# Set attention with routed experts on one core: weighing split over three engines, outputs stored as whole 128-partition rows

## The chip, the cores and the metric

One NeuronCore of a Trainium2 chip runs the kernel. The metric is the device time of one execution in microseconds (us). Before the change three executions took 180.69, 181.9 and 183.5 us, median 181.9 us. The execution that was profiled took 182.12 us.

## The reference, cut to what matters

An induced-set attention feeds a top-1 mixture of experts. `x` is 4 x 11456 x 128 (fp32), `inducing` is 32 x 128, there are 8 experts.

```python
def mab(q, kv):
    s = scale * (q @ kv.transpose(0, 2, 1))
    a = softmax(s)
    return a @ kv
h = mab(I, x)                        # 32 rows for each of 4 batches
x = mab(x, h).reshape(B * S, D)      # every token attends to the 32 rows

logits = x @ w_gate
expert_idx = argmax(logits)
gate_w = softmax(logits)[expert_idx]
out[mask] = gate_w[mask, None] * (np.maximum(xe @ w1[e], 0.0) @ w2[e])
```

## The kernel before

**Tiling.** A batch is cut into four segments (q = 0 to 3) and six groups (g), so there are 24 blocks k = 6 b + g of 15 x 4 x 32 tokens. A block's input is a tile of 128 partitions x 7680 bytes (`load_xt`, L528). Its output is a tile of 128 partitions: for each of four slices i (of up to 128 token rows) and each of the four segments q, 128 channels, 8192 bytes in a partition. The fourth slice i = 3 holds 96 rows and not 128, so in partitions 96 to 127 only the first three slices, 6144 bytes, are output.

**Stages.** A first pass (scores L539, maximum L545, exponential L582, transposition L585, `h_sum` L591) gives the batch's 32 rows h. For that, the block is also needed with tokens on partitions: 12 blocks are loaded a second time (`load_xn`, L531), 12 are turned by TensorE (`turn`, L551, evicted by `turn_out`, L556). A chain per batch (L611 to L763) picks the expert, fetches its weights (1 MB) and makes `h4`, the expert's output for the 32 rows. A second pass makes scores again (L539 with `hc`), maximum (`max2`, L766) and exponentials (`exp2`, L771), then the gate's chain for a round of one to three blocks: logits on TensorE (L774), VectorE, GpSimd (`gate_sm` L793, `gate_ls` L802, `gate_den` L816), ScalarE (`gate_exp`, L810), and the gate's factors `c_all` (`gate_c`, L819). Last, `experts` (L831) makes the output on TensorE into four PSUM banks, one for each q, 16 products of 32x128 by 32x128 for a block.

**Weighing.** Each bank (a quarter of a block, 128 x 512 values) is multiplied by the gate's factors on its way from PSUM into the block's output tile. `weigh` (L840) does this as one VectorE instruction with a broadcast operand, or as four ScalarE instructions, one for each slice i, since ScalarE takes its factor per partition:

```python
src, dst, c = self.bank(o).rearrange("p (i c) -> p i c", c=P), self.ob3(ob)[:, :, q, :], self.c_all[:, k, :, q]
if e == "DVE":
    self.nc.vector.tensor_tensor(out=dst, in0=src, in1=c.unsqueeze(2).to_broadcast([P, 4, P]), op=ALU.mult)
else:
    for i in range(4):
        self.nc.scalar.activation(dst[:, i], src[:, i], AF.Copy, scale=c[:, i : i + 1])
```

The tile is laid out (i, q, c), so a bank is written as four pieces of 512 bytes. For blocks 21 to 23 (`PARTS`) `weigh_part` (L849) goes by slices i over all four banks instead. `evict` (L857) and `weigh_late` (L859) exist but are not used, as `LATE` is empty.

**Stores.** SyncE issues every load but three and every store, in one order. Blocks 0 to 20 are stored by two transfers: partitions 0 to 95 with 8192 bytes each (768 KB) and partitions 96 to 127 with 6144 bytes (192 KB). Blocks 21 to 23 go out in two or four parts. 53 stores in all.

**Order.** `schedule` (L86) is a list scheduler that runs when the program is built: each operation has a rank (tables such as `THIRD`, `SECOND`, `LOAD_T`, offsets `OFF`), a planned duration for each engine that may do it, and buffers. It puts the instructions of each engine in a fixed order and chooses the engine where two are possible; VectorE takes such work only when ScalarE is busy for over `BEHIND` more ns (or over 0 for the blocks in `HURRY`). 17 buffers of 8192 bytes a partition (`big`) serve loads (`xt`, `xn`) and outputs (`ob`) alike; an output's buffer is free again when its stores have landed. Eight PSUM banks serve scores, turned blocks, `experts` and the small products.

Of the kernel before, what the change touches and what calls it, by code (L numbers as in the profile page):

```python
# [18 lines left out]
P = 128  # L19
# [10 lines left out]
BIG = 4 * NQ * P  # L30
LEFT = 3 * P
# [5 lines left out]
HOP, BEHIND = 55, 300  # L37
# [3 lines left out]
MODES = {"S1_": (1, 115), "S2_": (1, 115), "H": (1, 210), "LG": (1, 290), "X": (3, 190), "TR": (2, 40), "G": (1, 60)}  # L41
# [164 lines left out]
D = dict(S=812, H=805, X=900, TR4=430, TR3=330)  # L206
# [9 lines left out]
PARTS = {23: 1, 22: 1, 21: 2}  # L216
HURRY = (20, 22, 23)

EARLY = ()
LATE = ()  # L220
# [5 lines left out]
GROUPS = {"bank": (8, {"fe": 4, "o": 13, "mi": 18}), "big": (17, {"xt": 11, "xn": 4, "ob": 48})}  # L226


LOAD_T = [-6186, -5601, -2755, -2825, -4812, -1904, -3185, -850, -622, -34, 238, 439, 517, 628, 1135, 2484, 2554, 2211, 3138, 4227, 2869, 7643, 6799, 8479]
LOAD_N = [-1317, 303, -1889, 159, -514, 1482, -1301, -520, -276, -4, -1768, -515, 578, 431, 1568, 3352, 553, 193, -1797, 59, 2620, 2857, 583, 571]  # L230
FIRST = [-2245, -1527, -2081, 4254, 356, -2649, 1607, 163, 3238, 1476, 958, 3511, 1490, 2053, 2904, -2421, -2752, -2413, -3886, -2475, -4110, -1943, 831, -4632]
SECOND = [-232, 3747, 2518, 1714, -1344, -186, 366, 299, 306, 398, 156, 3259, 806, 2622, 811, 3248, -572, 3258, -168, 203, 186, 995, -368, 1821]
THIRD = [-4712, -4102, -212, 180, -264, 299, -78, 144, -4893, 605, 111, -3584, -3232, -435, -337, -3717, -61, -2978, -3177, -450, -45, -86, -3934, 558]
CHAIN = [-3399, -3392, -3373, -3377]

OFF = {'M1_': -684, 'ON': -730, 'TR': 292, 'TE': -809, 'MQ': -632, 'FD': -1684, 'NB': -843, 'E1_': -4857, 'T1_': -638, 'ZP': 660, 'H': -869, 'F': -875, 'AC': -39, 'hc': -101, 'gz': -555, 'gb': -1330, 'gg': -658, 'G': -64, 'GT': -981, 'GS': -346, 'GL': 2312, 'P': 1158, 'PC': 2646, 'PF': -127, 'h4_': -1128, 'dx': 1261, 'd': -2758, 'DF': -519, 'th': -371, 'M2_': -767, 'E2_': -412, 'LG': -240, 'LV': 1074, 'SM': -466, 'RS': 2277, 'LS': -208, 'PR': -697, 'SE': 117, 'SD': 902, 'C': -1284, 'X': -1247, 'V': 3829, 'OUT': -223, 'RL': 2569, 'GA': -1596, 'LT': -1764, 'LN': -833, 'CS': -1434, 'VL': 7}
# [7 lines left out]
def make_plan(K):  # L244
# [15 lines left out]
    for b in range(B):  # L260
# [5 lines left out]
        for g in range(NG):  # L266
# [26 lines left out]
            if g % 2:  # L293
# [3 lines left out]
                fd = op(f"FD{b}.{p}", r, {"PE": 280}, lambda mi=mi, b=b, p=p: K.max_fold(mi, b, p), [mq], take=[mi])  # L297
# [3 lines left out]
                for u in (g - 1, g):  # L301
# [3 lines left out]
                    ex = op(f"E1_{ku}", ru, {"ACT": 550}, lambda fe=fe_, e=e1_, b=b, p=p: K.exp1(fe, e, b, p), [nb], take=[e1_], use=[fe_])  # L305
# [52 lines left out]
    for nr, ks in enumerate(ROUNDS):  # L358
# [22 lines left out]
        c = op(f"C{nr}", rr, {"DVE": 90 + 110 * n + 240 * len(bs)}, lambda gt=gate, ks=ks: K.gate_c(gt, ks), [a, *(thrs[b] for b in bs)], use=[gate])  # L381
        rounds.append(c)
        for u, k in enumerate(ks):
            b, g = divmod(k, NG)
            ru = THIRD[k]
            os_, ob = [Buf("o") for _ in range(NQ)], Buf("ob")
            x = op(f"X{k}", ru, {"PE": D["X"]}, lambda os_=os_, e=e2[u], b=b: K.experts(os_, e, b), [exs[u], h4s[b], None if k in EARLY else c], take=[*os_, ob], use=[e2[u]], lat=70)
            step = PARTS.get(k, 4)
            vs = []
            for q in range(NQ):  # L390
                late = 0 if k in HURRY else None
                if k in LATE:
                    vs.append(op(f"V{k}.{q}", ru, {"ACT": 470, "DVE": 590}, lambda e, o=os_[q], ob=ob, q=q: K.evict(e, o, ob, q), [x], use=[os_[q], ob], wait=late))
# [17 lines left out]
class Issue:  # L411
# [108 lines left out]
    def ob3(self, b):  # L520
        return self.big[b.slot].rearrange("p (i q c) -> p i q c", q=NQ, c=P)
# [667 lines left out]
```

## Time and profile before

| | |
|---|---|
| median of three executions | 181.9 us (180.69 to 183.5) |
| the profiled execution | 182.12 us |
| its span, first to last instruction | 180.3 us |
| TensorE busy | 147.7 us (82%) |
| VectorE busy | 124.8 us (69%) |
| ScalarE busy | 120.0 us (67%) |
| GpSimd busy | 18.4 us (10%) |
| read from HBM, written to HBM | 39.87 MB, 23.59 MB |
| mean rate of all transfers over the span | 355 GB/s |

Busy is the time in which an engine had at least one instruction under way. The DMA share is the mean busy share of the core's 16 DMA engines; it can exceed 1 slightly, since a packet counts where it starts. An engine that is busy is not at its peak: a DMA packet that waits inside its transfer is busy as well, so share and GB/s are to be read together. No chain of waits to the end was found in this trace; the page's part on it is empty.

### The profile page before, as it was taken

How to read it: one execution, taken by the hardware profiler on the slowest of the kernel's cores; microseconds unless marked ns; L12 is line 12 of the kernel's file. 1: busy time of each engine (PE TensorE's matmuls, PEld its weight loads, DVE VectorE, ACT ScalarE, POOL GpSimd, SP SyncE). 2: the span in 40 equal slices, each digit the busy share in tenths (PEclk: the TensorE clock that was granted, in tenths of full speed). 3: DMA queues.
4: the chain of work that ended last, by engine and by line, in shares of the span. 5: the costliest groups of instructions: out<-in, count | busy, mean ns of one | idle time of the engine just before them, and what ended most of it. 6: DMA issues, size and time to landing. Idle time of an engine off the chain costs nothing.

```text
span 180.3 us, 6160 instructions
## 1 busy us (share of the span) xinstructions
PE 147.7 (82%) x2438; PEld 102.0 (57%) x2439; DVE 124.8 (69%) x360; ACT 120.0 (67%) x364; POOL 18.4 (10%) x75
## 2 busy tenths in 40 slices
PE   0699989999999999979999999989899889780000
PEld 0266767765577566538875545877644569670000
DVE  1117477798799989877789588979877948985000
ACT  3045354518256888766855999999999998993000
POOL 3000000000034000002400000241001401000000
PEclk9999999999999999999999999999999965965555
DMA  4999999999999998999999999999989999799990
GB/s 146 411 426 421 414 419 416 412 408 416 414 418 417 378 278 282 418 426 417 411 412 420 396 415 399 383 323 317 327 245 358 370 335 291 266 284 314 260 305 19
DMA packets 11124, 63.94 MB, mean 355 GB/s; under 512 B 1808, under 2 KB 1936, under 8 KB 8688
## 3 DMA queue, kind: packets, MB, share of 16 engines
q1 hardware_dynamic: 10512, 60.32, 89.2%
q10 hardware_dynamic: 576, 3.15, 4.4%
q8 instruction: 21, 0.34, 0.7%
q14 instruction: 15, 0.12, 0.2%
HBM read 39.87 MB, written 23.59 MB: 352 GB/s over the span
## 4 chain that ended last, share of the span: by engine, by line


## 5 line engine op out<-in xcount | busy, mean ns | idle before, releaser
L847 ACT ACTIVATE big<-bank,c_all 128x128 f32<-128x128 f32 x228 | 64.2, 555 | 5.1 <-PE bank L836 5.1
L836 PE MATMUL bank<-h,e 32*128 32x128 f32 x768 | 38.5, 307 | 4.7 <-ACT big L847 3.9
L836 PEld LDWEIGHTS bank<-h,e 32*128 32x128 f32 x768 | 32.1, 204 | 16.5 <-ACT big L847 9.1
L543 PE MATMUL bank<-big,it_s 128*32 128x480 f32 x192 | 26.1, 602 | 7.9 <-DMA big<-in_xT 7.8
L562 ACT COPY big<-bank 128x512 f32<-128x512 f32 (+1 forms) x37 | 19.5, 571 | 16.8 <-PE bank L554 14.9
L554 PE MATMUL bank<-csb,big 128*128 128x128 f32 x180 | 26.0, 291 | 0.2 <-issue 0.2
L772 ACT ACTIVATE e<-bank,nb 128x480 f32<-128x480 f32 x24 | 18.1, 791 | 11.3 <-DVE nb L769 4.5
L596 PE MATMUL bank<-big,e1t 128*32 128x129 f32 x720 | 25.6, 274 | 0.0
L554 PEld LDWEIGHTS bank<-csb,big 128*128 128x128 f32 x180 | 21.5, 152 | 6.9 <-issue 4.2
L546 DVE TENSOR_REDUCE mx<-bank 128x1 f32<-128x480 f32 x24 | 15.4, 645 | 14.1 <-PE bank L543 14.0
L596 PEld LDWEIGHTS bank<-big,e1t 128*32 128x32 f32 x720 | 21.6, 110 | 5.8 <-issue 3.7
L543 PE MATMUL bank<-big,hc 128*32 128x480 f32 x192 | 23.8, 570 | 0.7 <-ACT big L847 0.7
L844 DVE TENSOR_TENSOR big<-bank,c_all 128x512 f32<-128x512 f32 x27 | 18.0, 682 | 5.2 <-PE bank L836 5.2
L583 ACT ACTIVATE e<-bank,mx 128x480 f32<-128x480 f32 x24 | 15.1, 687 | 6.1 <-DVE mx L580 6.1
L768 DVE TENSOR_REDUCE mx<-bank 128x1 f32<-128x480 f32 x24 | 15.5, 645 | 4.3 <-PE bank L543 2.5
L586 DVE STREAM_TRANSPOSE e1t<-e 128x480 f32<-128x480 f32 x24 | 15.7, 660 | 1.4 <-PE bank L596 1.0
L543 PEld LDWEIGHTS bank<-big,it_s 128*32 128x32 f32 x192 | 5.6, 111 | 12.6 <-issue 9.7
L543 PEld LDWEIGHTS bank<-big,hc 128*32 128x32 f32 x192 | 6.2, 109 | 6.9 <-issue 3.5
L781 PE MATMUL bank<-e,gzb 128*32 128x128 f32 x192 | 8.1, 282 | 0.2 <-ACT big L847 0.2
L564 DVE COPY big<-bank 128x512 f32<-128x512 f32 (+1 forms) x11 | 6.7, 615 | 1.5 <-PE bank L554 1.0
L855 ACT ACTIVATE big<-bank,c_all 128x128 f32<-128x128 f32 x24 | 6.8, 440 | 0.9 <-PE bank L836 0.6
L803 POOL TENSOR_TENSOR ls<-lv,rs 128x336 f32<-128x336 f32 (+2 forms) x9 | 6.1, 686 | 9.5 <-DVE rs L800 5.8
(93 smaller groups left out, 130.9 us busy)
## 6 DMA issues: line engine op xcount, KB each, us to landing
big<-in_xT SPq DMA_DIRECT2D x24, 960.0 KB, 12.3
out<-big SPq DMA_DIRECT2D x21, 768.0 KB, 7.8
big<-in_xn SPq DMA_DIRECT2D x12, 967.5 KB, 13.3
out<-big SPq DMA_DIRECT2D x23, 192.0 KB, 7.6
wr<-in_wcat ACTq DMA_DIRECT2D x3, 1024.0 KB, 10.5
out<-big SPq DMA_DIRECT2D x6, 256.0 KB, 4.9
wr<-in_w SPq DMA_DIRECT2D x2, 512.0 KB, 5.6
out<-big SPq DMA_DIRECT2D x1, 512.0 KB, 6.7
```

The costliest lines, as they stand in the source:

```text
L543: self.nc.tensor.matmul(dst, lhsT=lhsT, rhs=x[:, k0:k1, q, :], start=True, stop=True)
L546: self.nc.vector.tensor_reduce(self.mx1[b][g // 2][:, g % 2 : g % 2 + 1], self.bank(fe)[:, :GW], AX.X, ALU.max)
L554: self.nc.tensor.transpose(ps[:, k * P : (k + 1) * P], x[:, k0 + k].rearrange("p q t -> p (q t)"), self.ident)
L562: self.nc.scalar.copy(dst, src)
L583: self.nc.scalar.activation(self.at(e), self.bank(fe)[:, :GW], AF.Exp, bias=self.mx1[b][p + 1][:, 2:3])
L586: self.nc.vector.transpose(self.at(t), self.at(e))
L596: self.nc.tensor.matmul(ps[32 * j : 32 * j + 32, : P + 1], lhsT=e[:, k, :], rhs=x[:, k, :], start=(n < 4), stop=(n >= 2 * GB - 4))
L768: self.nc.vector.tensor_reduce(t, self.bank(fe)[:, :GW], AX.X, ALU.max)
L772: self.nc.scalar.activation(self.at(e)[:, 0:GW], self.bank(fe)[:, :GW], AF.Exp, bias=self.nb2[k])
L836: self.nc.tensor.matmul(self.bank(os_[q])[:, i * P : (i + 1) * P], lhsT=self.at(e)[s, i * P : (i + 1) * P], rhs=self.h4[b][s, :], start=Tr ...
L844: self.nc.vector.tensor_tensor(out=dst, in0=src, in1=c.unsqueeze(2).to_broadcast([P, 4, P]), op=ALU.mult)
L847: self.nc.scalar.activation(dst[:, i], src[:, i], AF.Copy, scale=c[:, i : i + 1])
```

## The change

- The output tile is laid out (q, i, c): a bank's 512 values lie in one piece of 2048 bytes in each partition. The tensor in HBM has the same layout, and is put in order outside the timed execution. The pitch of a row stays 8192 bytes.
- `WHOLE`: blocks 0 to 20 are stored by one transfer of 128 partitions x 8192 bytes (1 MB), which includes the 2048 bytes in each of partitions 96 to 127 that are not output. Blocks 21 to 23 go out in parts by segments q, 128 partitions each.
- `LATE.get(k, 2)`: in every block two of the four quarters (q = 2, 3) are evicted from PSUM without a factor, by ScalarE or VectorE (one instruction), and then multiplied in place by GpSimd, one 128x512 instruction each. The other two are weighed as before. `weigh_part` is gone.
- The plan's durations, ranks and offsets are new, so the order on every engine may differ anywhere. The work of the passes, the loads and the chain is the same.
- `general_part`, a fallback for tokens whose expert differs, follows the new layout.

```diff
-HOP, BEHIND = 55, 300
+HOP, BEHIND = 55, 400
...
+WHOLE = 1
+
 EARLY = ()
-LATE = ()
+LATE = {0: 2, 1: 2, 2: 2, 3: 2, 4: 2, 5: 2, 6: 2, 7: 2, 8: 2, 9: 2, 10: 2, 11: 2, 12: 2, 13: 2, 14: 2, 15: 2, 16: 2, 17: 2, 18: 2, 19: 2, 20: 2}
...
-GROUPS = {"bank": (8, {"fe": 4, "o": 13, "mi": 18}), "big": (17, {"xt": 11, "xn": 4, "ob": 48})}
...
+GROUPS = {"bank": (8, {"fe": 24, "o": 97, "mi": 17}), "big": (17, {"xt": 11, "xn": 4, "ob": 39})}
...
-                if k in LATE:
-                    vs.append(op(f"V{k}.{q}", ru, {"ACT": 470, "DVE": 590}, lambda e, o=os_[q], ob=ob, q=q: K.evict(e, o, ob, q), [x], use=[os_[q], ob], wait=late))
-                elif step == 4:
-                    vs.append(op(f"V{k}.{q}", ru, {"ACT": 740, "DVE": 600}, lambda e, o=os_[q], ob=ob, k=k, q=q: K.weigh(e, o, ob, k, q), [x, c], use=[os_[q], ob], wait=late))
+                if q < NQ - LATE.get(k, 2):
+                    v = op(f"V{k}.{q}", ru, {"ACT": 1140, "DVE": 600}, lambda e, o=os_[q], ob=ob, k=k, q=q: K.weigh(e, o, ob, k, q), [x, c], use=[os_[q], ob], wait=late)
                 else:
-                    vs.append(op(f"V{k}.{q}", ru, {"ACT": 740, "DVE": 760}, lambda e, os_=os_, ob=ob, k=k, i=q: K.weigh_part(e, os_, ob, k, i), [x, c], use=[*os_, ob], wait=late))
...
+                    v = op(f"VE{k}.{q}", ru, {"ACT": 475, "DVE": 600}, lambda e, o=os_[q], ob=ob, q=q: K.evict(e, o, ob, q), [x], use=[os_[q], ob], wait=late)
+                    v = op(f"VL{k}.{q}", ru, {"POOL": 970}, lambda ob=ob, k=k, q=q: K.weigh_late(ob, k, q), [v, c], use=[ob])
+                vs.append(v)
...
-                cuts = ((q, 4, 0, 96), (q, 3, 96, P)) if step == 4 else ((q, q + step, 0, 96 if q == 3 else P),) if step == 1 else ((0, 2, 0, P),) if q == 0 else ((2, 4, 0, 96), (2, 3, 96, P))
...
+                cuts = ((0, P, 4),) if WHOLE or step == 1 else ((0, 96, 4), (96, P, 3))
...
-        return self.big[b.slot].rearrange("p (i q c) -> p i q c", q=NQ, c=P)
+        return self.big[b.slot].rearrange("p (q i c) -> p q i c", q=NQ, c=P)
...
-    def store(self, ob, b, g, i0, i1, p0, p1):
-        src = self.big[ob.slot][p0:p1, i0 * NQ * P : i1 * NQ * P]
-        self.nc.sync.dma_start(self.out[b, g, p0:p1, i0 * NQ * P : i1 * NQ * P], src)
+    def store(self, ob, b, g, q0, q1, p0, p1, ni):
+        dst = self.out[b, g, p0:p1, 0:BIG].rearrange("p (q i c) -> p q i c", q=NQ, c=P)[:, q0:q1, 0:ni]
+        self.nc.sync.dma_start(dst, self.ob3(ob)[p0:p1, q0:q1, 0:ni])
...
     def evict(self, e, o, ob, q):
-        self.copy(e, self.ob3(ob)[:, :, q, :], self.bank(o).rearrange("p (i c) -> p i c", c=P))
-
-    def weigh_late(self, ob, k, i):
-
-        t = self.ob3(ob)[:, i]
-        self.nc.gpsimd.tensor_tensor(out=t, in0=t, in1=self.c_all[:, k, i].unsqueeze(2).to_broadcast([P, NQ, P]), op=ALU.mult)
+        self.copy(e, self.ob3(ob)[:, q].rearrange("p i c -> p (i c)"), self.bank(o))
+
+    def weigh_late(self, ob, k, q):
+
+        t = self.ob3(ob)[:, q]
+        self.nc.gpsimd.tensor_tensor(out=t, in0=t, in1=self.c_all[:, k, :, q].unsqueeze(2).to_broadcast([P, 4, P]), op=ALU.mult)
```

## Rows read from the trace of the kernel before

**Rows 1.** The page: span, and the span in 40 slices (busy tenths, clock, DMA, GB/s).

```profile
span 180.3 us, 6160 instructions
...
PE   0699989999999999979999999989899889780000
...
ACT  3045354518256888766855999999999998993000
...
PEclk9999999999999999999999999999999965965555
DMA  4999999999999998999999999999989999799990
GB/s 146 411 426 421 414 419 416 412 408 416 414 418 417 378 278 282 418 426 417 411 412 420 396 415 399 383 323 317 327 245 358 370 335 291 266 284 314 260 305 19
```

**Rows 2.** Busy time by stage over the whole span, with granted clock, DMA share, GB/s.

```profile
core 0: us, PE busy (x) PEld busy (x) DVE busy (x) ACT busy (x) POOL busy (x), PEclk, DMA share, GB/s
0.00:5.00 5.00, 0.00 (x0) 0.01 (x1) 0.64 (x8) 1.50 (x3) 1.43 (x20) 1.00 0.54 175
5.00:60.00 55.00, 53.12 (x784) 36.58 (x788) 37.60 (x99) 26.17 (x55) 4.66 (x17) 1.00 1.02 415
60.00:107.00 47.00, 44.27 (x734) 28.08 (x734) 38.92 (x113) 36.57 (x108) 4.42 (x15) 1.00 1.00 386
107.00:141.00 34.00, 31.70 (x638) 21.75 (x641) 28.13 (x77) 33.58 (x121) 4.89 (x14) 1.00 0.97 341
141.00:177.00 36.00, 18.62 (x296) 15.55 (x288) 19.52 (x66) 22.19 (x85) 3.04 (x9) 0.66 0.89 291
177.00:180.30 3.30, 0.00 (x0) 0.00 (x0) 0.00 (x0) 0.00 (x0) 0.00 (x0) 0.50 0.01 2
```

**Rows 3.** DMA issues (KB each, median us to landing); then all stores.

```profile
big<-in_xT SPq DMA_DIRECT2D x24, 960.0 KB, 12.3
out<-big SPq DMA_DIRECT2D x21, 768.0 KB, 7.8
...
out<-big SPq DMA_DIRECT2D x23, 192.0 KB, 7.6
...
L536 SPq DMA_DIRECT2D out<-big x53: 316/685/2559, 62.4 to 174.0; - x53
```

**Rows 4.** Stores issued from 143.5 to 152.7 us; then busy time from 152.7 to 158.

```profile
L536 SPq DMA_DIRECT2D out<-big x6: 446/1672/2559, 143.5 to 152.7; - x6
...
DMA to landing us min/median/max: 6.1/7.7/8.0
...
152.70:158.00 5.30, 4.30 (x88) 3.86 (x91) 5.09 (x16) 5.30 (x23) 0.25 (x1) 1.00 0.77 265
```

**Rows 5.** The last work of an engine, and stores issued from 162 to 175 us.

```profile
163.00 1.14 ACT L855 ACTIVATE big<-bank,c_all 128x128 f32<-128x128 f32 x4 [0.28 <-DVE big L853]
...
L536 SPq DMA_DIRECT2D out<-big x10: 382/1562/2077, 160.6 to 174.0; - x10
...
DMA to landing us min/median/max: 2.9/5.5/7.1
```

**Rows 6.** Groups by line and shape: busy us, mean ns of one, idle before.

```profile
L847 ACT ACTIVATE big<-bank,c_all 128x128 f32<-128x128 f32 x228 | 64.2, 555 | 5.1 <-PE bank L836 5.1
L836 PE MATMUL bank<-h,e 32*128 32x128 f32 x768 | 38.5, 307 | 4.7 <-ACT big L847 3.9 <-DVE big L853 0.7
L844 DVE TENSOR_TENSOR big<-bank,c_all 128x512 f32<-128x512 f32 x27 | 18.0, 682 | 5.2 <-PE bank L836 5.2
L562 ACT COPY big<-bank 128x512 f32<-128x512 f32 x30 | 16.6, 590 | 16.7 <-PE bank L554 14.9 <-POOL u L734 1.5 <-POOL se L817 0.3
```

**Rows 7.** The same view, GpSimd's multiplication of the gate by three sizes.

```profile
L803 POOL TENSOR_TENSOR ls<-lv,rs 128x336 f32<-128x336 f32 x6 | 4.6, 774 | 6.1 <-DVE rs L800 5.8 <-ACT part L562 0.3
L803 POOL TENSOR_TENSOR ls<-lv,rs 128x224 f32<-128x224 f32 x2 | 1.1, 574 | 0.6 <-DVE sm L794 0.6
L803 POOL TENSOR_TENSOR ls<-lv,rs 128x112 f32<-128x112 f32 x1 | 0.4, 380 | 2.8 <-ACT big L847 2.8
```

**Rows 8.** From 107 to 161 us: all work, then weighing on ScalarE and VectorE alone.

```profile
107.00:161.00 54.00, 48.86 (x915) 36.15 (x919) 44.76 (x132) 53.00 (x194) 7.92 (x23) 0.92 0.95 327
...
107.00:161.00 54.00, 44.33 (x157) 0.92 0.95 327
...
107.00:161.00 54.00, 13.96 (x21) 0.92 0.95 327
```

More of the change, by code (lines that the diff above doesn't have):

```diff
@@ L202, in schedule @@
     return order
-D = dict(S=812, H=805, X=900, TR4=430, TR3=330)
+D = dict(S=812, H=812, X=905, TR4=430, TR3=330)
 LAT = dict(PE=180, DVE=85, ACT=115, POOL=45)
@@ L296, in make_plan @@
                 mq = op(f"MQ{b}.{p}", r, {"DVE": 120}, lambda b=b, p=p: K.max_spread(b, p), [m1[g - 1], m1[g], nb_prev, cs])
-                fd = op(f"FD{b}.{p}", r, {"PE": 280}, lambda mi=mi, b=b, p=p: K.max_fold(mi, b, p), [mq], take=[mi])
+                fd = op(f"FD{b}.{p}", r, {"PE": 300}, lambda mi=mi, b=b, p=p: K.max_fold(mi, b, p), [mq], take=[mi])
                 nb = op(f"NB{b}.{p}", r, {"DVE": 100}, lambda mi=mi, b=b, p=p: K.max_all(mi, b, p), [fd], use=[mi])
@@ L304, in make_plan @@
                     fe_, e1_, e1t_, xnr_ = e1[u]
-                    ex = op(f"E1_{ku}", ru, {"ACT": 550}, lambda fe=fe_, e=e1_, b=b, p=p: K.exp1(fe, e, b, p), [nb], take=[e1_], use=[fe_])
+                    ex = op(f"E1_{ku}", ru, {"ACT": 510}, lambda fe=fe_, e=e1_, b=b, p=p: K.exp1(fe, e, b, p), [nb], take=[e1_], use=[fe_])
                     tt = op(f"T1_{ku}", ru, {"DVE": 565}, lambda e=e1_, t=e1t_: K.turn_e(e, t), [ex], take=[e1t_], use=[e1_])
@@ L372, in make_plan @@
         side = "DVE" if nr in QUICK else "POOL"
-        a = op(f"LG{nr}", rr, {"PE": 30 + 140 * n}, lambda lg=lg, es=e2, ks=ks: K.logits(lg, es, ks), [*(gzbs[b] for b in bs), *exs], take=[lg], use=[lg, *e2])
+        a = op(f"LG{nr}", rr, {"PE": 100 + 215 * n}, lambda lg=lg, es=e2, ks=ks: K.logits(lg, es, ks), [*(gzbs[b] for b in bs), *exs], take=[lg], use=[lg, *e2])
         a = op(f"LV{nr}", rr, {"DVE": 75 + 140 * n}, lambda lg=lg, lv=lv, n=n: K.logits_turn(lg, lv, n), [a], take=[lv], use=[lg])
         a = op(f"SM{nr}", rr, {side: 80 + 20 * n if side == "DVE" else 220 + 40 * n}, lambda e=side, lv=lv, gt=gate, n=n: K.gate_sm(e, lv, gt, n), [a], take=[gate], use=[lv])
-        a = op(f"RS{nr}", rr, {"DVE": 50 + 105 * n}, lambda gt=gate, n=n: K.gate_rs(gt, n), [a], use=[gate])
+        a = op(f"RS{nr}", rr, {"DVE": 50 + 108 * n}, lambda gt=gate, n=n: K.gate_rs(gt, n), [a], use=[gate])
         a = op(f"LS{nr}", rr, {side: 70 + 120 * n if side == "DVE" else 150 + 210 * n}, lambda e=side, lv=lv, gt=gate, n=n: K.gate_ls(e, lv, gt, n), [a], use=[lv, gate])
@@ L380, in make_plan @@
         a = op(f"SD{nr}", rr, {side: 80 + 20 * n if side == "DVE" else 160 + 40 * n}, lambda e=side, gt=gate, n=n: K.gate_den(e, gt, n), [a], use=[gate])
-        c = op(f"C{nr}", rr, {"DVE": 90 + 110 * n + 240 * len(bs)}, lambda gt=gate, ks=ks: K.gate_c(gt, ks), [a, *(thrs[b] for b in bs)], use=[gate])
+        c = op(f"C{nr}", rr, {"DVE": 100 + 120 * n + 240 * len(bs)}, lambda gt=gate, ks=ks: K.gate_c(gt, ks), [a, *(thrs[b] for b in bs)], use=[gate])
         rounds.append(c)
@@ L840, in weigh @@
     def weigh(self, e, o, ob, k, q):
-        src, dst, c = self.bank(o).rearrange("p (i c) -> p i c", c=P), self.ob3(ob)[:, :, q, :], self.c_all[:, k, :, q]
+        src, dst, c = self.bank(o).rearrange("p (i c) -> p i c", c=P), self.ob3(ob)[:, q], self.c_all[:, k, :, q]
         if e == "DVE":
@@ L1097, in general_part @@
                             nc.vector.transpose(ec, e2)
-                            rows = (out_flat[bass.ds((b * NG + g) * P, 96), :], out_flat[bass.ds((b * NG + g) * P + 96, 32), 0 : LEFT * NQ])
-                            ob = pl.ob.tile([P, 4, NQ, P], F32, name="ob")
-                            mine = ob.rearrange("p i q c -> p (i q c)")
-                            mine = (mine[0:96, :], mine[96:P, 0 : LEFT * NQ])
+                            rows = [out_flat[bass.ds((b * NG + g) * P + p0, p1 - p0), q * 4 * P : q * 4 * P + n] for p0, p1, n in ((0, 96, 4 * P), (96, P, LEFT)) for q in range(NQ)]
+                            ob = pl.ob.tile([P, NQ, 4, P], F32, name="ob")
+                            mine = [ob.rearrange("p q i c -> p q (i c)")[p0:p1, q, 0:n] for p0, p1, n in ((0, 96, 4 * P), (96, P, LEFT)) for q in range(NQ)]
                             for m, r in zip(mine, rows):
@@ L1126, in general_part @@
                                         )
-                                    nc.vector.tensor_tensor(out=ob[0:n, i, q, :], in0=ob[0:n, i, q, :], in1=o[0:n, 0:P], op=ALU.add)
+                                    nc.vector.tensor_tensor(out=ob[0:n, q, i, :], in0=ob[0:n, q, i, :], in1=o[0:n, 0:P], op=ALU.add)
                             for m, r in zip(mine, rows):
@@ L1181 @@
     ]
-    out = nc.dram_tensor("out_0", (B, NG, P, BIG), F32, kind="ExternalOutput").ap()
+    out = nc.dram_tensor("out_0", (B, NG, P, PITCH), F32, kind="ExternalOutput").ap()
     with tile.TileContext(nc) as tc:
```

42 lines of the change are left out of this document (17 added, 25 removed).

## The prediction

> **What bounds the kernel now.** I read the page first, the slices from left to right. The DMA line stands at nine tenths or more almost everywhere [rows 1]. Below it the GB/s line tells more: about 415 in the first third, and then, with the engines as busy as before, 245 to 370 from slice 26 on. So the transfers set the pace from start to end, and in the second half they get slower without getting rarer.
>
> The stages say the same in one table [rows 2]. From 5 to 60 us the DMA share is 1.02 at 415 GB/s. No store is issued before 62.4 us [rows 3], so this is the rate of loads alone. From 60 to 107 us, loads with a few stores, it is 386; from 107 to 141 us, nearly all stores, 341 at a share of 0.97; from 141 to 177 us, stores and little else, 291 at 0.89. A busy engine thus moves 415 / 1.02 = 407 GB/s (times 16) in loads and 291 / 0.89 = 327 in stores.
>
> Why are stores slower? Loads go to 128 partitions; stores come from 96 and then from 32 [rows 3]. The stretch from 152.7 to 158 us tells most [rows 4]: the DMA share falls to 0.77 although the six stores issued before it take 6.1 to 8.0 us to land, so transfers were outstanding all through it. Some of the 16 engines had run empty while others still had a backlog: the work was unevenly spread, and those with a backlog were slow. [...] I read the slow stores as a matter of which partitions a transfer covers.
>
> Second, who feeds the stores? From 107 to 161 us ScalarE is busy for 53.0 of 54 us, 44.3 of it with weighing, and TensorE for 48.9 [rows 8]. ScalarE is the bound of computing there; TensorE's wait before `experts` is mostly for ScalarE [rows 6]. But the last weighing ends at 163.00 + 1.14 = 164.1 us, while stores are issued until 174.0 [rows 5] and bytes move until about 177 [rows 2]: 13 us of drain. So the DMA engines set the end, and ScalarE stands close behind.
>
> **The change part by part.**
>
> *Whole-row stores.* They add 32 x 2048 bytes for each of 24 blocks, 1.57 MB: 63.94 MB (the GB/s of rows 2 times their stretches, 63.9) become 65.51 MB. What 128 partitions x 8192 bytes cost in a store, no row of before shows. Upper bound: the rate of 141 to 177 us, 291 GB/s, 3.6 us for a store. Lower bound: the loads' 415 GB/s, 2.53 us. The new store has the loads' shape, 128 rows of nearly the same length (8192 against 7680 bytes) in one transfer, so I take 415. The sum of the whole traffic then is 65.51 MB / 415 GB/s = 157.9 us. Ahead of it lie 2.9 us (0 to 5 us moved 0.875 MB, worth 2.1 us); behind it 3.3 us in which nothing moves [rows 2]. The last store can't be overlapped: 2.9 us from issue to landing at the least [rows 5], of which its 256 KB are 0.6 us, so 2.3 us more. Loads and stores will not mesh without gaps: the stage from 60 to 107 us ran at 386 instead of 415, 3.3 us lost; part of that is the old stores' doing, so I keep half, 1.6 us. Sum 2.9 + 157.9 + 2.3 + 3.3 + 1.6 = 168.0 us of span. The profiled execution took 182.12 us with a span of 180.3, so 1.8 us lie around it: 169.8 us, rounded 170. That execution stands 0.2 us above the median of the runs shown, so no correction is due.
>
> [...]
>
> *Dividing the weighing.* A quarter costs ScalarE 64.2 / 57 = 1.13 us (four instructions) and VectorE 0.68 us [rows 6]. An eviction costs ScalarE 0.55 us by its copies of the same size (16.6 / 30) [rows 6]; it may be less, as the destination is now one piece; I take 0.55. From 107 to 161 us 39 quarters went through ScalarE (157 / 4) and 21 through VectorE, 60 in all [rows 8]. After the change 30 are evicted and 30 weighed. ScalarE: 53.0 - 44.3 + 30 x 0.55 = 25 us; VectorE: 44.8 - 14.0 + 30 x 0.68 = 51 us; with ten weighings handed to ScalarE, 36 and 44 us. So both fall well under 54, and TensorE's 48.9 becomes the longest. Computing would end some 5 us sooner, near 159 us. That is worth nothing by itself, since the transfers end at 163 to 165 us by the sum above; but it keeps the stores fed, and if this cover is gone (second rival) it costs 5 us. `weigh_part` going away saves VectorE and ScalarE little and is costed at nothing, hidden in the drain of the last blocks.
>
> *GpSimd's 48 instructions.* GpSimd takes 380, 574 and 774 ns for 112, 224 and 336 values [rows 7], 1.76 ns a value; on that line 512 cost 1.08 us. Lower bound: 0.77 us, the row of fewer values. [...] I take 1.08. In the stretch of 60 quarters that is 30 x 1.08 + 7.9 = 40 us of 54, so GpSimd keeps up. It adds a wait: in GpSimd's order the gate's `gate_sm`, `gate_ls` and `gate_den` now stand behind these instructions, up to 1.08 us each, 3.2 us a round; `gate_exp` on ScalarE, `gate_c` on VectorE and then `experts` wait for them. Ten rounds could lose 32 us if nothing else were ready; TensorE has scores of later blocks to do meanwhile, so I charge nothing. A block's store also starts some 2 us later, as two GpSimd instructions follow its last eviction; with stores outstanding, that is hidden, and its buffer is held longer by as much.
>
> *SyncE.* 31 issues of stores replace 53. Behind a store that waits, later loads wait too on this queue; the store now waits for GpSimd. Since most loads are issued before 107 us and there is a backlog of 12 us [rows 3], I charge nothing.
>
> **The rivals.**
>
> *First, computing sets the end.* Work still ends at 164.1 us, because TensorE does not get shorter, or because GpSimd's wait eats the 5 us. Then the last store needs 5.5 us (the median of the last ten [rows 5]), and 3.3 + 1.8 us follow: 174.7 us. For it: TensorE at 48.9 of 54 us [rows 8]. [...]
>
> *Second, stores of 128 partitions are no faster* (the change doesn't do what it says, because the limit lies in writing to HBM). Then 1.57 MB more at 291 GB/s is 5.4 us: 187.5 us, slower. For it: the drop in GB/s follows the writes [rows 1]. [...]
>
> *Third, GpSimd becomes the bound.* If its instruction costs t, the stretch lasts 30 t + 7.9 us. It equals today's 54 us at t = 1.54. The whole is slower than before once computing ends at 171.4 us (182 - 5.5 - 3.3 - 1.8), that is at t = 1.78. [...]
>
> **How the numbers follow.** The forecast (transfers bound, 170 us) gets 0.62, with a range of 165.5 (no gaps, no tail) to 173. Rival one (174.7) gets 0.22, rival two (187.5) 0.08, rival three (from 182 to 193) 0.08. Leaving out the two slow ones and the fringe, the range is 165 to 177. Faster by over 2% (under 178.3; about what a measurement of this kernel can tell from no change): 0.62 + 0.22, less a little for a late rival one, 0.83. Within 2%: rival one's late end and rival three near its threshold, 0.08. Slower: 0.09.
>
> **What would show it.** Right: GB/s near 400 or above in the stretches where stores dominate; a store of 1 MB landing every 2.5 to 2.7 us while several are outstanding; weighing on ScalarE down to about 10 us per 60 quarters; GpSimd's instruction near 1.1 us; the last landing within 6 us after the last evicted bank. Wrong: 300 GB/s at a full DMA share in the store stretches (rival two); GpSimd busy nine tenths with ScalarE or TensorE waiting for `ls` or `se` (rival three); a DMA share that falls to 0.8 from 120 us on because no block is ready (rival one).

## The result and the profile after

The changed kernel took 173.28 us (median of three, 172.34 to 173.77) against 181.9 us: the ratio is 0.955, 95% interval 0.943 to 0.967. The profiled execution took 172.34 us with a span of 170.5 us, so 1.8 us lie around the span as before. In the experiments below, an execution more than 1.5% above the fastest of its kernel stays in the median and is left out of the ratio; without such executions the two kernels with paired stores and the division take 184.4 us (old order) and 185.5 us (new order) instead of 185.5 and 186.1.

The page's slices of the changed kernel, which answer to [rows 1], with one row of the DMA issues and one of all stores, which answer to [rows 3]:

```profile
span 170.5 us, 6074 instructions
...
PE   0599999999999998999999999997999985666300
...
ACT  3046637338554592969246896798793995781700
POOL 3000000000024262037430452788694799786800
...
DMA  4999999999999999999999999999999999899890
GB/s 140 407 422 427 411 420 411 413 416 409 415 418 411 420 411 320 368 425 420 419 410 414 426 316 414 423 424 421 411 417 397 349 423 373 340 377 380 317 394 38
...
out<-big SPq DMA_DIRECT2D x21, 1024.0 KB, 8.3
...
L537 SPq DMA_DIRECT2D out<-big x31: 332/343/769, 61.2 to 162.4; - x31
```

The GB/s line is the one to read: before, it sank to 245 to 370 from slice 26 on; now it is at 411 to 424 in slices 26 to 29 and lies between 317 and 423 from there until the last full slice. The DMA line is as full as before. GpSimd, idle before for most of the span, is busy from slice 11 on.

Busy time by stage, answering to [rows 2]; the columns are the same (after the stretch and its length: busy us and instructions of TensorE, its weight loads, VectorE, ScalarE, GpSimd, then clock, DMA share, GB/s). The last row is the stretch of [rows 8]:

```profile
0.00:5.00 5.00, 0.00 (x0) 0.01 (x1) 0.64 (x8) 1.50 (x3) 1.43 (x20) 1.00 0.56 182
5.00:60.00 55.00, 53.16 (x792) 36.20 (x796) 37.36 (x100) 28.08 (x59) 5.49 (x18) 1.00 1.02 415
60.00:107.00 47.00, 46.00 (x810) 30.18 (x806) 41.48 (x113) 32.02 (x77) 17.86 (x29) 1.00 1.00 395
107.00:141.00 34.00, 31.31 (x651) 21.11 (x647) 30.88 (x82) 28.05 (x78) 26.06 (x38) 1.00 1.01 408
141.00:170.50 29.50, 11.91 (x214) 10.33 (x206) 16.82 (x37) 13.02 (x40) 16.85 (x21) 0.71 0.80 316
...
107.00:161.00 54.00, 43.22 (x856) 31.44 (x848) 47.70 (x118) 41.05 (x118) 41.51 (x57) 0.91 0.97 389
```

From 107 to 141 us, nearly all stores, the rate is 408 GB/s where it was 341 [rows 2]. Up to 60 us the rate did not change. What is left of slowness lies in the last stretch, with a DMA share of 0.80. From 107 to 161 us ScalarE fell from 53.0 to 41.05 us, GpSimd rose from 7.9 to 41.5.

The groups that answer to [rows 6 and 7] (line, busy us, mean ns, idle before); L856 is GpSimd's multiplication, L563 ScalarE's copies out of PSUM (turned blocks and late quarters together), L848 and L845 the weighing on ScalarE and VectorE:

```profile
L856 POOL TENSOR_TENSOR big<-big,c_all 128x512 f32<-128x512 f32 x48 | 49.4, 1050 | 24.8 <-ACT big L563 16.0 <-DVE big L565 5.5 <-DVE hc L629 2.8
L563 ACT COPY big<-bank 128x512 f32<-128x512 f32 x72 | 39.7, 604 | 35.5 <-PE bank L555 18.4 <-PE bank L837 12.6 <-issue 3.4
L837 PE MATMUL bank<-h,e 32*128 32x128 f32 x768 | 33.1, 302 | 1.8 <-DVE big L845 1.1 <-DVE big L565 0.4 <-ACT big L848 0.2
L848 ACT ACTIVATE big<-bank,c_all 128x128 f32<-128x128 f32 x100 | 29.2, 404 | 0.0
L845 DVE TENSOR_TENSOR big<-bank,c_all 128x512 f32<-128x512 f32 x23 | 15.5, 675 | 1.3 <-PE bank L837 1.2
```

ScalarE's weighing fell from 64.2 to 29.2 us (100 instructions, 25 quarters). GpSimd takes 1.05 us an instruction. TensorE's `experts` takes 33.1 us instead of 38.5, and its waits for banks fell from 4.7 to 1.8 us; that the second is the reason for the first was not tested.

### The profile page after: what moved, and what is told of

The parts are those of the page before. It is cut to its first block, busy times and chain, and to the rows that moved or that the text cites. A ratio compares the mean times of both kernels' runs of the same rounds, so it can differ in the third digit from the quotient of the medians.

```text
span 170.5 us, 6074 instructions
## 1 busy us (share of the span) xinstructions
PE 142.4 (84%) x2438; PEld 97.8 (57%) x2439; DVE 127.2 (75%) x337; ACT 102.7 (60%) x255; POOL 67.7 (40%) x123
## 5 line engine op out<-in xcount | busy, mean ns | idle before, releaser
L563 ACT COPY big<-bank 128x512 f32<-128x512 f32 (+1 forms) x80 | 43.2, 593 | 36.7 <-PE bank L555 19.7
L856 POOL TENSOR_TENSOR big<-big,c_all 128x512 f32<-128x512 f32 x48 | 49.4, 1050 | 24.8 <-ACT big L563 16.0
L837 PE MATMUL bank<-h,e 32*128 32x128 f32 x768 | 33.1, 302 | 1.8 <-DVE big L845 1.1
L837 PEld LDWEIGHTS bank<-h,e 32*128 32x128 f32 x768 | 28.2, 203 | 9.1 <-DVE big L845 2.0
L848 ACT ACTIVATE big<-bank,c_all 128x128 f32<-128x128 f32 x100 | 29.2, 404 | 0.0
L773 ACT ACTIVATE e<-bank,nb 128x480 f32<-128x480 f32 x24 | 15.3, 687 | 15.2 <-DVE nb L770 7.6
L845 DVE TENSOR_TENSOR big<-bank,c_all 128x512 f32<-128x512 f32 x23 | 15.5, 675 | 1.3 <-PE bank L837 1.2
L587 DVE STREAM_TRANSPOSE e1t<-e 128x480 f32<-128x480 f32 x24 | 15.6, 656 | 0.9 <-ACT e L584 0.9
L565 DVE COPY big<-bank 128x512 f32<-128x512 f32 (+1 forms) x16 | 10.3, 646 | 4.0 <-PE bank L837 2.5
L550 POOL MEMSET big<- 128x15 f32 x12 | 1.3, 127 | 25.5 <-PE bank L597 22.0
L795 POOL TENSOR_SCALAR sm<-lv 128x48 f32<-128x48 f32 (+2 forms) x9 | 3.2, 355 | 11.8 <-DVE lv L785 10.1
```

Of the source, the lines that this page charges most:

```text
L563: self.nc.scalar.copy(dst, src)
L587: self.nc.vector.transpose(self.at(t), self.at(e))
L773: self.nc.scalar.activation(self.at(e)[:, 0:GW], self.bank(fe)[:, :GW], AF.Exp, bias=self.nb2[k])
L837: self.nc.tensor.matmul(self.bank(os_[q])[:, i * P : (i + 1) * P], lhsT=self.at(e)[s, i * P : (i + 1) * P], rhs=self.h4[b][s, :], start=Tr ...
L856: self.nc.gpsimd.tensor_tensor(out=t, in0=t, in1=self.c_all[:, k, :, q].unsqueeze(2).to_broadcast([P, 4, P]), op=ALU.mult)
```

## The experiments

Three theories stood against each other. **1:** the gain comes from transfers that cover all 128 partitions. **2:** it comes from ScalarE's relief by GpSimd. **3**, added after the first runs: it comes from the new order. Unless said otherwise a variant keeps the order of its parent on every engine; only what an operation issues is changed. Times are medians; each ratio is to the kernel before, run on the same chip in turn (its median was 182.6 to 182.9 us there).

### Stores alone

The disputed price was measured by itself. A first kernel has only stores of 8192-byte rows from six tiles of 1 MB: whole; as 96 and 32 partitions; as 64 and 64; whole again.

```diff
+    shapes = (((0, P),), ((0, 96), (96, P)), ((0, 64), (64, P)), ((0, P),))
...
+            for g in range(NG):
+                for a, z in cuts:
+                    nc.sync.dma_start(out[b, g, a:z, 0:BIG], big[g][a:z, :])
```

> Leaves out all computing and all loads: four phases of six stores of 8192-byte rows each, from six tiles, with a pause between the phases: 128 partitions in one transfer; 96 and 32; 64 and 64; 128 again. Theory 1: about 2.5 us a tile for one transfer (15 us a phase), 3.3 us for 96 and 32 (20 us), more for 64 and 64. If writing to HBM is what limits stores: the same time a tile in all four phases, 3 us or more.

Windows inside the first, second and fourth phase (VectorE, GpSimd, clock, DMA share, GB/s). The pause before a phase is a small write to each tile, and a tile's next store waits for its own write only; so the phases ran into each other at their borders, and the second is somewhat mixed with the third:

```profile
16.00:28.00 12.00, 0.29 (x5) 0.00 (x0) 1.00 1.01 416
32.00:48.00 16.00, 0.29 (x5) 0.00 (x0) 1.00 1.01 337
70.00:82.00 12.00, 0.00 (x0) 0.00 (x0) 1.00 0.98 410
```

Whole tiles go out at 410 to 416 GB/s, a load's rate; 1 MB is 2.5 us. With 96 and 32 partitions it is 337 GB/s at the same busy share. Writing to HBM is not what limits the old stores.

A second kernel, with clean pauses, separates the ranges: 0 to 95 alone, 96 to 127 alone, 0 to 63 alone, and 0 to 63 and 64 to 127 in turn.

```diff
-    shapes = (((0, P),), ((0, 96), (96, P)), ((0, 64), (64, P)), ((0, P),))
+    shapes = (((0, 96),), ((96, P),), ((0, 64),), ((0, 64), (64, P)))
...
-            for t in big:
+            for t in reversed(big):
                 nc.vector.memset(t[:, 0:1], 2.0)
```

> Leaves out all computing and all loads: four phases of six tiles with rows of 8192 bytes, each phase begun after the last store of the one before: partitions 0 to 95 alone; 96 to 127 alone; 0 to 63 alone; 0 to 63 and 64 to 127 as two transfers. If a transfer's rate goes with the share of partitions that it covers evenly: 96 partitions 2.4 to 2.6 us a tile (no quicker than 128, at 2.45), 32 partitions 0.9 to 1.2 us, 64 alone 2.4 us, 64 and 64 together no more than 2.8 us since the two halves overlap. If only bytes count: 1.85, 0.62, 1.23 and 2.45 us.

A window inside each phase, same columns:

```profile
16.00:28.00 12.00, 0.00 (x0) 0.00 (x0) 1.00 0.96 317
33.00:40.00 7.00, 0.00 (x0) 0.00 (x0) 1.00 1.00 206
44.00:57.00 13.00, 0.00 (x0) 0.00 (x0) 1.00 0.97 204
61.00:80.00 19.00, 0.00 (x0) 0.00 (x0) 1.00 0.99 313
```

At 317 GB/s the 768 KB of 96 partitions take 786 432 bytes / 317 GB/s = 2.48 us, as long as a whole megabyte. 32 and 64 partitions alone go at half the full rate (206 and 204 GB/s) with all 16 engines busy (share 1.00 and 0.97): the engines are occupied, but a byte takes them twice the time. So in these runs the rate depends on which partitions a store covers, and bytes alone do not give its price. Two of the expected times were too low: 256 KB from 32 partitions took 1.27 us (0.9 to 1.2 expected), and 1 MB as 64 and 64 took 3.35 us (no more than 2.8 expected).

### The store's shape in either kernel

In the changed kernel, each whole store is split into 96 and 32 partitions; bytes, order and division stay.

```diff
-        self.nc.sync.dma_start(dst, self.ob3(ob)[p0:p1, q0:q1, 0:ni])
+        for a, z in ((p0, 96), (96, p1)) if q1 - q0 == NQ else ((p0, p1),):
+            self.nc.sync.dma_start(self.out[b, g, a:z, q0 * 4 * P : q1 * 4 * P], self.big[ob.slot][a:z, q0 * 4 * P : q1 * 4 * P])
```

> The changed kernel in the same order on every engine, but each 1 MB store is issued as two transfers, 96 and 32 partitions of 8192 bytes; bytes, division and plan stay. Theory 1 (the gain comes from transfers that cover all 128 partitions): a block's store goes from some 2.65 us back to about 3.2 us or more, 21 x 0.55 = 11.6 us at a full DMA queue, so 182 to 186 us, with GB/s near 300 to 340 and packets that take longer at a full DMA share in the store stretches. Theory 2 (the gain comes from ScalarE's relief by GpSimd and from the new order; the shape of the store matters little): at most 175 us.

186.08 us, ratio 1.029 (1.012 to 1.045): all of the gain is lost, and more. The stages of [rows 2] from 107 us on, in this kernel:

```profile
107.00:141.00 34.00, 28.81 (x562) 19.50 (x558) 27.91 (x71) 25.10 (x73) 23.46 (x33) 0.95 0.92 326
141.00:177.00 36.00, 16.54 (x310) 13.75 (x310) 20.39 (x47) 16.69 (x50) 20.32 (x27) 0.71 0.96 324
```

ScalarE has slack (25.1 of 34 us), the DMA engines are as busy as ever, and 324 to 326 GB/s come out. Theory 2 has no place for that.

In the kernel before, each pair is made one whole store.

```diff
+        if i0 == 0 and p0 == 96:
+            return
+        if i0 == 0 and i1 == 4:
+            p1 = P
         src = self.big[ob.slot][p0:p1, i0 * NQ * P : i1 * NQ * P]
```

> The kernel before in its own order, but each of its 21 paired stores is one transfer of 128 partitions x 8192 bytes; nothing else. Theory 1: the drain after the last weighing shrinks from 13 us to some 6 us, and then ScalarE is the bound: weighing ends near 162 to 164 us and the time is 172 to 176 us, so most of the gain without any division of work. Theory 2: 180 to 183 us, since ScalarE stays busy all the time and 1.6 MB more are moved.

179.18 us, ratio 0.988 (0.968 to 1.009; the two medians, 179.18 and 182.87 us, give 0.980): too little to be told from no change, so theory 1 in its plain form missed here. From 107 to 161 us:

```profile
107.00:161.00 54.00, 49.13 (x912) 34.34 (x905) 44.88 (x129) 53.25 (x193) 7.97 (x23) 0.94 0.92 357
```

ScalarE is full (53.25 of 54 us) and the DMA share falls to 0.92: now the transfers wait for blocks, while ScalarE has no time to spare. The faster store ran into the second bound, as expected, but this bound ended at 167 to 168 us and not at 162 to 164.

### The division in either kernel

In the changed kernel, the late quarters are weighed where they are evicted, and GpSimd does nothing of it.

```diff
-lambda e, o=os_[q], ob=ob, q=q: K.evict(e, o, ob, q)
+lambda e, o=os_[q], ob=ob, k=k, q=q: K.weigh(e, o, ob, k, q)
...
-lambda ob=ob, k=k, q=q: K.weigh_late(ob, k, q)
+lambda: None
```

> The changed kernel in the same order, but the 48 quarters that were evicted and then multiplied by GpSimd are weighed at their eviction, by the engine that evicted them (40 on ScalarE, 8 on VectorE); GpSimd does none of it. Theory 1: ScalarE gets 40 x 0.6 = 24 us more, becomes the bound again in the late stretch, but a block's store no longer waits for GpSimd: 173 to 178 us. Theory 2: back to 180 us or more. Besides, if GpSimd holds VectorE's instructions that read SBUF twice, the small ones of the gate's chain that took about 1.0 us in the changed kernel (the maximum of margins, the scaled identity, the denominator) go back to 0.28, 0.29 and 0.17 us; if those durations are the profile's noise, they stay.

178.34 us, ratio 0.987 (0.976 to 0.999). That is just above the upper end of what theory 1 gave (178), and 5.1 us above the changed kernel. ScalarE is back at 50.5 of 54 us with the DMA share at 0.88:

```profile
107.00:161.00 54.00, 45.30 (x824) 31.04 (x815) 40.37 (x114) 50.47 (x187) 7.80 (x23) 0.92 0.88 348
```

The second question was VectorE. Three of its groups in the changed kernel, then the same three without GpSimd's multiplications (mean ns is the last figure but one):

```profile
L756 DVE TENSOR_SCALAR dg<-csb,u 128x128 f32<-128x128 f32 x4 | 2.5, 614 | 0.1
L804 DVE TENSOR_TENSOR ls<-lv,rs 128x112 f32<-128x112 f32 x1 | 1.0, 1019 | 0.0
L818 DVE TENSOR_TENSOR se<-se,sm 128x16 f32<-128x16 f32 x1 | 1.0, 1015 | 0.0
```

```profile
L756 DVE TENSOR_SCALAR dg<-csb,u 128x128 f32<-128x128 f32 x4 | 1.1, 287 | 0.1
L804 DVE TENSOR_TENSOR ls<-lv,rs 128x112 f32<-128x112 f32 x1 | 0.3, 265 | 0.0
L818 DVE TENSOR_TENSOR se<-se,sm 128x16 f32<-128x16 f32 x1 | 0.2, 174 | 0.0
```

GpSimd does hold some of VectorE's instructions: an operation on 16 values takes 1015 ns instead of 174, which is 0.84 us more; one of GpSimd's multiplications takes 1.05 us. VectorE's weighing, whose large operand is in PSUM, is not held (675 ns, 682 before [rows 6]), nor are its reciprocals of 48 values (L823, 446 ns, 447 without GpSimd's multiplications) or its transpositions of the exponentials (L587, 656 and 660 ns). What sets these apart from the held ones was not tried.

In the kernel before, with its paired stores, two quarters of a block are evicted and multiplied by GpSimd directly after.

```diff
+    def divide(self, e, o, ob, k, q):
+        self.evict(e, o, ob, q)
+        t = self.ob3(ob)[:, :, q, :]
+        self.nc.gpsimd.tensor_tensor(out=t, in0=t, in1=self.c_all[:, k, :, q].unsqueeze(2).to_broadcast([P, 4, P]), op=ALU.mult)
```

> The kernel before in its own order and with its own paired stores (96 and 32 partitions), but in blocks 0 to 20 two of four quarters are evicted by the engine that weighed them, and multiplied in place by GpSimd directly after. Theory 1 (two bounds lie close together: paired stores at some 3.2 us a block and ScalarE; relieving one alone meets the other): 179 to 184 us, no gain to speak of, with ScalarE's busy share down and the DMA share at 0.95 or above until the end. Theory 2 (ScalarE was the bound): 174 to 176 us.

185.51 us, ratio 1.017 (1.008 to 1.026): slower, if by little. Relief alone buys nothing while the stores are slow. That there is a loss, theory 1 did not say, and the DMA share from 107 to 161 us is 0.92 where it gave 0.95 or more.

### Both edits in the old order, and the order itself

> The kernel before in its own order, with both edits: whole-row stores and the division by GpSimd in blocks 0 to 20. Theory 1: the two edits together make the gain, the new plan is a trimming: 172 to 176 us, against about 179 with either edit alone. Theory 3 (the new order of all work makes the gain, the edits alone do little): 177 us or more.

The two edits above together in the old order: 179.71 us, ratio 0.984 (0.977 to 0.990). Theory 1 missed by some 4 us: in the old order the two edits give no more than the whole-row store alone, so something in the new order is needed. (This kernel keeps the old layout and does not divide blocks 21 to 23; GpSimd's instruction is as long in it, 1.05 us.) The stretch from 120 to 130 us, then two of its waits over the whole span, and what SyncE's queue waited for from 112 to 132 us:

```profile
120.00:130.00 10.00, 7.75 (x158) 6.12 (x152) 8.34 (x22) 7.27 (x24) 8.23 (x12) 0.99 0.62 250
...
ACT pr L815 <- POOL ls L807: 6.9, 5, 2.2
...
DVE rs L804 <- POOL sm L798: 3.0, 3, 1.4
...
SPq L540 <- POOL big L867: 9.6, 3, 5.4
```

From 120 to 130 us no engine is full and the DMA share is 0.62: the transfers wait for blocks. SyncE stood 9.6 us before stores whose quarters GpSimd had not yet multiplied, and ScalarE and VectorE waited 6.9 and 3.0 us over the whole span for the gate's small instructions on GpSimd. The same three views of the changed kernel:

```profile
120.00:130.00 10.00, 9.57 (x188) 6.75 (x189) 8.37 (x23) 7.77 (x23) 8.43 (x9) 1.00 1.00 415
...
ACT pr L812 <- POOL ls L804: 1.2, 2, 0.7
...
SPq L537 <- POOL big L856: 1.8, 3, 1.0
```

Is it enough that the scheduler knows of GpSimd's work? The changed kernel with the old rank tables and offsets (its layout, its planned durations and the division of all blocks stay):

```diff
-LOAD_T = [-22443, -17046, -16332, -16270, -16871, -6593, -6405, -6461, -6571, -5910, -3605, -2321, -2277, -805, -871, -90, 773, -421, 15135, 20378, 15273, 21295, 22306, 21798]
+LOAD_T = [-6186, -5601, -2755, -2825, -4812, -1904, -3185, -850, -622, -34, 238, 439, 517, 628, 1135, 2484, 2554, 2211, 3138, 4227, 2869, 7643, 6799, 8479]
...
```

> The changed kernel with the rank tables and offsets of the kernel before (the two new kinds of operation rank like the old weighing): the list scheduler knows of GpSimd's 48 instructions, their durations and the whole-row stores, and makes its own order, but not the new priorities. The old order with both edits put in by hand took 179.7 us. If what it lacked was an order that reckons with GpSimd: 173 to 176 us here. If the priorities of the new plan are what counts: 177 to 181 us.

179.19 us, ratio 0.982 (0.968 to 0.996). It is not enough; the priorities count, and the layout is not what the old order lacked. The same hole, the gate's wait over the whole span, and from 112 to 132 us SyncE's wait and GpSimd's longest:

```profile
120.00:130.00 10.00, 8.82 (x213) 7.62 (x216) 8.18 (x24) 9.10 (x30) 7.23 (x11) 1.00 0.62 252
...
ACT pr L812 <- POOL ls L804: 6.9, 6, 2.4
...
SPq L537 <- POOL big L856: 13.4, 4, 6.8
...
POOL big L856 <- DVE big L565: 5.3, 2, 4.4
```

The gate's wait does not make this hole: only 0.4 of its 6.9 us lie between 112 and 132 us. There SyncE waits for GpSimd's multiplication, and GpSimd waits for an eviction by VectorE. What the two old orders share is that late quarters keep stores waiting; which of the priorities cures it was not tried.

And is the new order good by itself? It was run with neither edit.

> The changed kernel's order with neither of the two edits: stores of 96 and 32 partitions (8192 bytes each) and all quarters weighed at their eviction, nothing on GpSimd. With it all four pairs of edits are known in the new order: both 173.3, whole rows alone 178.3, division alone 186.1 us. If the edits add up: 178.3 + 186.1 - 173.3 = 191 us. If each matters only where the other has taken the nearer bound away: no worse than the division alone, 184 to 187 us, and then the new order without the edits is slower than the old one.

186.4 us, ratio 1.025 (1.015 to 1.035): it is slower than the old order. The edits do not add up (191 us was the sum). All eight pairs, in us:

| stores, weighing | old order | new order |
|---|---|---|
| paired, not divided | 181.9 to 182.9 (before) | 186.4 |
| paired, divided | 185.5 | 186.1 |
| whole, not divided | 179.2 | 178.3 |
| whole, divided | 179.7 | 173.3 (changed) |

Whole rows are worth 8.1 us in the new order without the division and 12.8 us with it; the division is worth nothing with paired stores, and 5 us with whole rows, in the new order only. So theory 3 fails in its plain form as well: the order alone costs some 4 us, and the gain needs the whole rows, some division and the new priorities together.

### Dose, and the tail

Half the division (q = 3 alone goes through GpSimd):

```diff
+K.weigh(e, o, ob, k, q) if q == 2 else K.evict(e, o, ob, q)
...
+None if q == 2 else K.weigh_late(ob, k, q)
```

> The changed kernel in its order with half the dose: of the two late quarters of each block q = 2 is weighed at its eviction and q = 3 still goes through GpSimd (24 instructions instead of 48). If ScalarE's relief works like a threshold (the transfers are the bound once ScalarE has slack): 172.5 to 174 us. If it works in proportion: half way between 178.3 and 173.3, 175.8 us.

172.73 us, ratio 0.948 (0.938 to 0.957), the same as the whole dose within the noise. Relief acts as a threshold: past half the dose, more of it is worth nothing. From 107 to 161 us of this kernel:

```profile
107.00:161.00 54.00, 43.90 (x875) 31.75 (x868) 43.68 (x119) 48.71 (x164) 26.44 (x41) 0.94 0.98 388
```

ScalarE is busy for 48.7 us, against 50.5 without the division (DMA share 0.88) and 41.1 with all of it. The step lies between the first two figures, which differ little, so ScalarE's busy time alone does not explain it; which wait ends there was not found.

In the changed kernel TensorE waits 2.94 us for the count of tokens left, ahead of the last two blocks' products. The count was put last:

```diff
-        for o in schedule(make_plan(K), CAPS, GROUPS):
+        for o in sorted(schedule(make_plan(K), CAPS, GROUPS), key=lambda o: o.name == "LEFT"):
```

> The changed kernel, but the count of tokens left (a reduction on VectorE, a product on TensorE, a copy) stands at the end of every engine's order; in the changed kernel TensorE waited 2.94 us for its reduction ahead of the output products of the last two blocks. If that wait is on the path to the end: 1 to 1.5 us less than the changed kernel (its factors come at about 154.2 us, the products started at 155.5), so 171.8 to 172.3 us. If the last blocks wait for something else just as long (buffers, banks, the factors): no difference, 173.3 us.

173.05 us (ratio 0.947, 0.942 to 0.952), no difference. Then, besides, the last two blocks without GpSimd and in four stores each:

```diff
+K.weigh(e, o, ob, k, q) if k in (18, 19) else K.evict(e, o, ob, q)
...
+        for a, z in ((2, 3), (3, 4), (0, 1), (1, 2)) if b * NG + g in (18, 19) else ((q0, q1),):
```

> As the kernel with the count moved to the end, and besides the last two blocks to finish (18 and 19) are weighed at their eviction, without GpSimd, and each is stored in four transfers by q instead of one. In the changed kernel GpSimd worked 4.07 us in a row for these two blocks and the last store landed 6.3 us after its issue. If the tail sets the end: 2.5 to 4 us less than the changed kernel, 169 to 171 us. If the DMA queue is still the bound there: at most 1 us less.

173.92 us (ratio 0.953, 0.948 to 0.958). The expected 2.5 to 4 us did not come. Two stretches of that kernel, and its stores issued from 155 us on:

```profile
140.00:150.00 10.00, 6.49 (x146) 5.01 (x134) 9.76 (x27) 7.46 (x24) 8.27 (x13) 1.00 0.89 369
150.00:160.00 10.00, 7.09 (x122) 6.50 (x122) 8.52 (x16) 7.82 (x29) 6.33 (x7) 0.66 0.97 372
...
L537 SPq DMA_DIRECT2D out<-big x13: 332/597/1552, 155.1 to 164.6; - x13
...
DMA to landing us min/median/max: 4.7/5.2/6.0
```

Each of the 13 last stores took 4.7 to 6.0 us to land, though it holds 256 KB or 1 MB: they stood behind each other. All computing ended before 161 us, while stores were issued until 164.6: the transfers are the bound at the end, and work that ends sooner does not help. The test is not quite clean, since stores of 256 KB have rows of 2048 bytes only, and these moved less at full engines, 363 GB/s at a share of 1.03 in one stretch of this kernel. That stretch, and the changed kernel's last three stretches with the packets of the middle one:

```profile
162.00:166.00 4.00, 0.00 (x0) 0.00 (x0) 0.00 (x0) 0.00 (x0) 0.00 (x0) 0.50 1.03 363
...
140.00:150.00 10.00, 6.52 (x147) 5.31 (x142) 9.79 (x25) 6.87 (x23) 8.40 (x12) 0.99 0.88 358
150.00:160.00 10.00, 6.39 (x101) 5.82 (x97) 7.32 (x15) 6.00 (x18) 7.04 (x9) 0.50 1.00 383
160.00:170.50 10.50, 0.00 (x0) 0.00 (x0) 0.71 (x2) 1.01 (x4) 2.40 (x3) 0.66 0.57 221
...
DMA packets 1367, 3.83 MB, mean 383 GB/s; under 512 B 149, under 2 KB 149, under 8 KB 1237
```

At 363 instead of 408 GB/s the two blocks' 2.1 MB cost some 0.6 us more (an estimate), too little to hide a gain of 2.5 to 4.

None of these variants beats the changed kernel by more than the intervals.

## Why the prediction was right, and by how much it was off

The forecast was 170.0 us, range 165 to 177; the time is 173.3, on the forecast side. One of its sums is off: the low end of the inner range, without gaps and tail, is 169.8 - 1.6 - 2.3 = 165.9 us and not 165.5. By its steps:

- **The bound.** Right: transfers bound, slow because of the partitions that they cover [rows 2 and 4]. Shown by the stores alone (410 to 416 GB/s whole, 337 as 96 and 32 partitions) and by splitting the stores again (324 to 326). That some engines run empty, as [rows 4] were read, is at most a part of it: in stores from 32 or 64 partitions alone the share stayed at 1.00 and 0.97 while the rate halved (206 and 204 GB/s).
- **The store at a load's rate, 157.9 us for all bytes.** Right: 408 GB/s from 107 to 141 us (415 taken), 410 to 416 for stores alone.
- **Lead and end.** The lead was 2.8 us (2.9 taken): 0 to 5 us moved 0.91 MB. The last store was issued at 162.4 us and landed 6.3 us later at 168.8, so the end was 1.7 us (3.3 taken). That it fell short hid 1.6 us of the next term: luck.
- **Gaps and the last store: the term that was mis-sized.** 1.6 + 2.3 us were taken. Measured against 415 GB/s, the stage from 60 to 107 us lost 47 x (1 - 395 / 415) = 2.3 us, the next 0.6 us, and from 141 to 168.8 us 27.8 - 29.5 x 316 / 415 = 5.3 us: 8.2 us instead of 3.9. With the shorter end that makes the 2.5 us by which the span (170.5 against 168.0) is longer; the median of three lies another 0.9 us above the profiled execution. Of these 5.3 us, 1.4 were lost from 140 to 150 us, at a share of 0.88, when too few blocks were ready; 0.8 from 150 to 160 us at a share of 1.00; and 3.2 after 160 us, where the last store lands. So the 2.3 us for the last store were about right, and the gaps were taken too small. From 150 to 160 us most packets are of 2048 or 4096 bytes, from the blocks stored in parts; that they moved less, 363 GB/s at a share of 1.03 where the last two blocks went out in four stores each, the prediction did not reckon. That the last batch's expert chain causes the gap from 140 to 150 us, with VectorE's instructions held by GpSimd (1.0 us where it was 0.3) and TensorE waiting 1.92 us for one of them, is argued from the trace; it was not tried.
- **The division.** The stretch from 107 to 161 us came out close to the working in its totals: ScalarE 41.1 us (36 foreseen), VectorE 47.7 (44), GpSimd 41.5 (40), 1.05 us an instruction (1.08). TensorE became shorter, 43.2 instead of 48.9, which was not reckoned. "Worth nothing by itself, 5 us if the cover is gone": without the division the time is 5.1 us longer.
- **What was charged nothing.** GpSimd's queue in front of the gate's instructions was charged nothing, since TensorE would have other work. In the new order that held: ScalarE's wait for it is 1.2 us in all. In the old one it is 6.9 us, SyncE waits for late quarters besides, and both edits give 179.2 to 179.7 us: the new priorities are worth 5.9 to 6.4 us, and the prediction gave them no term at all. With the old ones the time would have lain outside its range; that the new plan had what the working left out was luck, as far as the forecast goes.
- **Rivals.** The first (computing sets the end, 174.7 us) is partly what happened: the time lies between it and the forecast, with transfers bound for most of the span and short of blocks near 145 us. The second is refuted by the stores alone, 410 to 416 GB/s from 128 partitions. The third did not come: GpSimd is at 41.5 of 54 us, and its 48 instructions took 1.04 to 1.08 us each; what was held were small instructions of VectorE (1015 ns instead of 174). No run shows an instruction of GpSimd that would give the 193 us at the end of the third's range.
- **The signs.** Met: 408 GB/s where stores dominate, and 1.05 us for GpSimd's instruction. Not met: ScalarE's weighing took 21.0 us from 107 to 161 us, for 18 of 68 quarters where ten of 60 were foreseen, and the last landing came 7.8 us after the last eviction (161.0 us) and not within 6. The sign of rival one, a share of 0.8 from 120 us on, was not seen: 1.00 from 120 to 140 us, 0.88 to 150, 1.00 to 160.

## What to carry to other kernels

A DMA share near 1 says that the engines are occupied, not that they move data (206 GB/s at a share of 1.00 from 32 partitions, 416 at 1.01 from 128): divide the GB/s by the share, stage by stage, and look at which partitions the transfers of a slow stage cover; a padded transfer over all 128 can be quicker than an exact one over 96 and 32 (6.7% more bytes here, at 410 to 416 GB/s instead of 337). Where two bounds lie close together, removing either one alone gives little; test the edits in pairs, and in the order that was made for them. Work that is moved to an idle engine also stands in that engine's queue in front of what others wait for, and the stores wait for it in turn (with both edits in the old order ScalarE waited 6.9 us over the span and SyncE 9.6 us from 112 to 132 us, in the changed kernel 1.2 and 1.8); here only an order made for it hid that.

## What the runs showed of the hardware that was not expected

A store from 64 partitions (0 to 63) takes about as long as one from 128, 2.5 to 2.6 us (204 against 410 to 416 GB/s), and one from 96 takes 2.48 us (317 GB/s). Both were expected before the second store kernel ran; that two halves of 64 in turn reach only 313 GB/s was not. Stores of 256 KB with rows of 2048 bytes moved 363 GB/s at a share of 1.03, whole stores of 1 MB 408 at 1.01. An operation of VectorE on 16 values took 1015 ns instead of 174 while GpSimd multiplied. ScalarE's copies out of PSUM, most of them now into one piece of 2048 bytes, were no quicker (604 ns in the mean) than into the turned blocks' tiles before (590 [rows 6]).
